# Half-word copies of 32 weight tiles moved to VectorE, units 4 to 9 turned by TensorE, new constants in the program's layout

## The chip, the cores and the metric

The kernel runs on one core of a Trainium2 chip. The metric is device time in microseconds (us) of one execution; the lower, the better. A core has a matrix engine (TensorE, PE in the rows; PEld is its weight load), VectorE (DVE), ScalarE (ACT), GpSimd (POOL) and SyncE (SP), which issues nearly all DMA transfers here. Each engine works through its own instructions in order.

## The reference

Three layers follow each other: attention over a window of 64 positions, a layer with squared relu, and a layer with a softmax gate and a normalization.

```python
# q, k, v: (4, 8, 576, 64)
scores = scale * q @ k^T;  mask: 0 <= i - j < 64
attn = softmax(scores) @ v                      # -> x: (2304, 512)
h = max(x @ w_in, 0);  x = h * h @ w_out        # (512, 2048), (2048, 512)
h = x @ w2_in                                   # (512, 1024)
s = h * softmax(h);  ln = (s - mean(s)) / sqrt(var(s) + 1e-6) * g_ln
out = ln @ w2_out                               # (1024, 512)
```

Activations are 32-bit floats. The four weight matrices come as 64-bit floats.

## The kernel before

**Weights.** A weight tile is 128 x 512. `assembled` loads its 64-bit words as they are (`load`, 512 KB, tile `wraw`), shifted by one 16-bit word, and makes 32-bit floats of them in two steps: `top` (L247, ScalarE) copies the highest half-word of each, read as bf16 and written as f16, into a word of the tile `top` (one of two that are used in turn) or straight into the result; `rest` (L250, VectorE) shifts the other bits and joins both. The 16 tiles of w_in (kind `a`, result `w`) and the 16 of w_out (kind `b`, result `wm`) go through `top`. For the second layer's weights (kinds `2i` and `2o`, 8 tiles each) GpSimd first clears the result (`home`, L235). `weights` then splits a tile into a high and a low part (L266 on ScalarE, L269 on VectorE), since each product is made of three (high times high and both mixed ones).

**Attention.** The 36 blocks of 64 positions are taken two at a time: 18 units. A unit is: load q and k (L372, L373), scores on TensorE (L418, `ps_s`), mask and maximum on VectorE (L421, L426), exponentials on ScalarE (L443), normalization (`norm`, L453, on VectorE for units 0 to 9 and on GpSimd after), a turn of the probabilities `e`, and the product with v (`values`, L511, `ps_v`). Units 0 to 3 are turned by TensorE (L471, `ps_p`) and copied out of PSUM by ScalarE (L489, `pt`). From unit 4 (`CROSSED = 4`) VectorE turns blocks of 32 x 32 (`blocks`, L477, tile `d`), and two transfers finish the turn through memory: `aside` (L480, 512 KB to `p_dram`) and `across` (L485, four of 128 KB into `pt`). From unit 4 on the result `xt` is stored (L533).

**Squared-relu layer.** Units 0 to 3 are pass 0: `ffn` multiplies by w_in (L688, `ps_h`) and w_out (L704, `ps_y`), hidden tile after hidden tile, while the later units run in between; 51 products without use (`ps_warm`, L1492) stand in the order early on. Units 4 to 9 are pass 2, units 10 to 17 pass 3. These use seven products in place of eight (`pair1`, L914, `ps_h`; sums `u2`, `u3`, `c22`, `c21`, `c12` on VectorE at L930, L934, L942, L945, L949, tiles `u1`, in rows `u` or `u_` with a number) for each pair j of hidden tiles. Their operands are sums and splits of x (`x_operands`) and of weights (`w_operands`, L854 to L867, tiles `ws`, `wo`, `wz`). `squares_of` squares on GpSimd (L622) and splits (L634 on ScalarE, L637 on VectorE); `second` multiplies by w_out (L1031). The hidden tiles go to memory and come back for the second half (`again_of`). The tag `wm` is a ring of four tiles, shared by `xt`, the sums and the weights of kind `b` and `2i`.

**Last layer.** `pair2` and `behind` (L1303, L1427 to L1449).

**Order.** All of this is laid out once, in Python: `add(engine, us, rank, function, after, take, give, port, late, at)` records a task, and `plan.run` picks again and again the task that could start first by these costs (ties by rank). `late` is what a transfer is assumed to take beyond its issue, `port` marks VectorE and GpSimd work that is assumed to exclude each other, `take` and `give` are slots of tiles. The result is a fixed order on each engine. On the chip only waits on data decide when an instruction of that order starts.

Of the kernel before, what the change touches and what calls it, by code (L numbers as in the profile page):

```python
# [26 lines left out]
class Plan:  # L27
# [71 lines left out]
def kernel(  # L99
# [92 lines left out]
    with ExitStack() as c1:  # L192
# [22 lines left out]
        def assembled(kind, i, rank, after=()):  # L215
            early = kind == "a" and i < EARLY
            ringed = kind in "ab"
            o = {}

            def load():  # L220
                o["raw"] = raw_p.tile([P, 1024], I32, tag="wraw", name="wraw", bufs=RAWS)
                nc.sync.dma_start(out=o["raw"].bitcast(U16)[:, : 4 * DM - 1], in_=SRC[kind][i][:, 1:])

            def home():
                if kind == "a":
                    if i // 2 not in w1:
                        w1[i // 2] = w1_p.tile([P, 2, 512], F32, tag="w1", name="w1")
                    o["m"] = w1[i // 2][:, i % 2]
                elif kind == "2o":
                    w2o[i] = w1_p.tile([P, 2, 512], F32R, tag="w1", name="w2o")  # L230
                    o["m"] = at_p.tile([P, 512], F32, tag="qk"[i % 2], name="w2m", bufs=1)
                else:
                    o["m"] = raw_p.tile([P, 512], F32, tag="wm", name="wm", bufs=WMB)
                if not ringed:
                    G.memset(o["m"], 0.0)  # L235

            def top():
                if ringed:
                    home()
                    if not tops:  # L240
                        tops.append(x_p.tile([P, 2, 512], F32, tag="xc", name="top", bufs=1))
                        G.memset(tops[0], 0.0)
                    o["t"] = tops[0][:, turns[0] % 2]
                    turns[0] += 1
                else:
                    o["t"] = o["m"]
                S.activation(out=o["t"].bitcast(F16)[:, 1::2], in_=o["raw"].bitcast(BF16)[:, 2::4], func=AF.Copy)  # L247

            def rest():
                V.scalar_tensor_tensor(out=o["m"].bitcast(I32), in0=o["raw"][:, ::2], scalar=13, in1=o["t"].bitcast(I32),  # L250
                                       op0=ALU.logical_shift_right, op1=ALU.bitwise_or)

            a = add("SP", 1.7, rank - (LEAD if early else 9), load, after, take=["raw"], late=2.0, at=0.7)
            own = {"a": [], "2o": ["qk"[i % 2] + "2"]}.get(kind, ["wm"])
            z = [] if ringed else [add("POOL", 0.6, rank - 9, home, after, take=own, port=True)]
            b = add("ACT", 0.57, rank, top, [a, *z], take=["top", *own] if ringed else [])
            return o, add("DVE", 0.62, rank, rest, [b], port=True, give=["raw", "top"] if ringed else ["raw"])

        def weights(kind, i, rank, after=()):
# [48 lines left out]
        def landed(lo, source, after, rank, n):  # L308

            def load():  # L310
                nc.sync.dma_start(out=lo[0]().bitcast(F32), in_=source())

            return add("SP", 0.8, rank - 6, load, [*after, *lo[2]], take=lo[1], late=2.2)

        def less(lo, a, b, after, rank, n, op=ALU.subtract):

# [22 lines left out]
        def attention(n, rank, after=()):  # L339
# [246 lines left out]
            else:  # L586
# [5 lines left out]
                    p = [add("PE", 0.85, rank, lambda: transposes(0), [*ns, before], take=["t", "t", "pt"], give=["e"])] * 2  # L592
                if crossed:
                    c = add("DVE", 1.2, rank, blocks, ns, take=["raw"], give=["e"], port=True)
                    c = add("SP", 0.8, rank, aside, [c], late=2.4, give=["raw"])
                    c = [add("SP", 1.6, rank, across, [c, before], take=["pt"], late=2.4)]
                else:
                    c = [add("ACT", 0.48, rank, lambda a=a: copied(a), [p[a]], give=["a" if begins else "t"]) for a in range(2)]
                p = add("PE", 1.15, rank, lambda: values(0), [*c, lv], take=["t"], give=["pt", vs])
                if t < 2:  # L600
                    h = add("ACT", 0.48, rank, lambda: high(0), [p])
                    x_ready[n] = add("DVE", 0.60, rank, lambda: rest(0), [h], give=["t"])
                else:
                    h = add("ACT", 0.48, rank, taken, [p], take=["wm"], give=["t"])
                    x_ready[n] = add("SP", 0.8, rank, store_x, [h], late=2.2, give=["wm"])
            p_after[n] = p


# [21 lines left out]
        def squares_of(o, N, rank, done, late=False, signed=True, turn=()):  # L630

            def high():
                o["g"] = g_p.tile([P, 2, NMAX], F32R, tag="g", name="g")
                S.activation(out=o["g"][:, 0, :N], in_=o["r"], func=AF.Copy)  # L634

            def rest():
                V.tensor_tensor(out=o["g"][:, 1, :N], in0=o["r"], in1=o["g"][:, 0, :N].bitcast(F32), op=ALU.subtract)  # L637

            e = squared(o, N, rank, done, late, signed)
            o["task"] = s = add("ACT", N / 1200 + 0.11, rank, high, [e, *turn], take=["g"])  # L640
            return add("DVE", N / 960 + 0.07, rank, rest, [s], port=True, give=[o["slot"]] if o["slot"] else [])
# [404 lines left out]
                        freed[dh] = got  # L1046
                        gone[t, half, dh] = got

        twin = {}

        def again_of(t, kk, at, unit, pos=None, last=None):
            N, half = HN[t], int(t > 1)
            base = next((b for b in TWINS if half and kk - b in (0, 1)), None)
            twice = base is not None
            o = {"slot": "raw" if twice else "wm" if kk > 3 and kk % 4 == 3 else "r"}
# [20 lines left out]
            else:  # L1076
# [2 lines left out]
                else:  # L1079
                    begun = [in_of[0, KF - 1 - AGO, 0]]  # L1080
                a = add("SP", 0.8, at - SOON - EARLIER, load, [r_ready[t, kk], *begun], take=[o["slot"]], late=3.5)
            e = squares_of(o, N, at - (FIRST if half and kk < 3 else SOON), [a], late=LATE_POOL and t == LAST, signed=None if half else False, turn=last_square[t][-2:][: 1 + kk] if half and kk < 2 else last_square.get(t, [])[-1:])
            if twice and kk > base:
                e["after"].append(twin["e"])
            twin["e"] = e
# [12 lines left out]
                return dict.__getitem__(self, k)  # L1098

        PAIR0, PAIR = 10.88, 8.6  # L1100
        JOIN, SECOND, MORE = 4, 0.17, PASSES[1]
        SKIP = 6 if MORE else KF

# [2 lines left out]
        V0, LATER, OUT = 3.12, 52.7, 4.55  # L1106
        LEAD = 14.41
        SOON, EARLIER, LATE_POOL = 25, 0, False
        PUT, PUT0, PUT1, AGO, LATEB, WOP = 16, 10, 3, 0, 145, 11
        TWINS, PAIRED, AHEAD, TWINJ = (3, 9), 2, 7, 7  # L1110
        NEXT, FIRST, ENDS = 20, 8, 70
        UNIT = (1.68, 2.12, 15.1, 22.97)
        WIDE, EAGER, CROSSED = 18, starts[3] // 2, 4
        W2I, W2O, XOP, KW = 11.0, 7.0, -15, 40
        NOT2I = lambda: first_of[2, 4]
        for n, (kind, kk) in enumerate((kind, kk) for kk in range(KF) for kind in "ab"):
            weights(kind, kk, LATEB + 3 * (kk - PUT) if kind == "b" and kk >= PUT else LOADS[n] if n < len(LOADS) else PAIR0 + PAIR * n / 2 - 2)
# [427 lines left out]
```

## Time and profile before

| | |
|---|---|
| median of 3 runs | 670.98 us (668.65 to 671.6) |
| profiled execution, its own time | 664.84 us |
| its span, first to last instruction | 662.8 us |
| TensorE busy | 634.9 us, 96% |
| VectorE busy | 494.8 us, 75% |
| ScalarE busy | 399.5 us, 60% |
| GpSimd busy | 129.6 us, 20% |

The profiled execution took 664.84 us, of which 2.0 us lie around the span. Of the span, TensorE stood still for 27.9 us, all but 5.2 us of it in the first 313 us.

### The profile page before, as it was taken

What the parts mean: (1) busy time and instruction counts of PE and PEld (TensorE: products, weight loads), DVE (VectorE), ACT (ScalarE), POOL (GpSimd) and SP (SyncE); (2) the same over time, 40 slices, a digit from 0 to 9 for tenths busy, and PEclk for the clock granted to TensorE, in tenths of its full rate; (3) what the DMA queues carried; (4) which work ended last, traced back from release to release, by engine and by line L of the source; (5) the groups of instructions that cost most, each with busy time, mean ns of one, the idle gap of its engine ahead of it and who ended that gap; (6) DMA issues with size and microseconds to landing.
All of it is one profiled execution on the core that took longest, in us unless ns stands there. A gap on an engine that the chain in (4) does not pass through costs nothing.

```text
span 662.8 us, 11290 instructions
## 1 busy us (share of the span) xinstructions
PE 634.9 (96%) x4041; PEld 532.4 (80%) x4041; DVE 494.8 (75%) x846; ACT 399.5 (60%) x899; POOL 129.6 (20%) x164
## 2 busy tenths in 40 slices
PE   8999998899898989999999999999999999999997
PEld 4678877688797889898888888888888787778786
DVE  5879878698985974379877674388888798787761
ACT  6877677658755833475555544564565666566652
POOL 1003022034324343101433333200000000000000
PEclk9999999999999989999999999999999999999999
DMA  8787998834878667765222113562165534565221
GB/s 285 262 309 249 285 321 297 257 105 146 267 221 262 211 199 227 266 238 167 84 87 92 66 64 142 193 202 67 49 189 176 183 116 125 149 191 157 105 72 48
DMA packets 75672, 118.18 MB, mean 178 GB/s; under 512 B 6880, under 2 KB 46304, under 8 KB 75616
## 3 DMA queue, kind: packets, MB, share of 16 engines
q1 hardware_dynamic: 75072, 117.20, 53.9%
q8 instruction: 32, 0.52, 0.3%
q10 hardware_dynamic: 544, 0.26, 0.1%
q14 instruction: 24, 0.20, 0.1%
HBM read 79.16 MB, written 38.27 MB: 177 GB/s over the span
## 4 chain that ended last, share of the span: by engine, by line
PE 48%; DVE 2%; DMA 1%; ACT 1%; issue 1%; SPq 0%; ACTq 0%; DVEq 0%
PE ps_o L1444 13%; PE ps_y L1031 13%; PE ps_h L1303 11%; PE ps_h L914 11%; DVE lnT L1437 1%; DMA l<-t_dram 1%; DVE e L1387 0%; DVE h L1404 0%; DVE nmax L1376 0%; ACT lnT L1433 0%; PE ps_lt L1427 0%; SPq L1413 0%; ACT h L1325 0%; ACT o L1449 0%; DVE h L1334 0%
## 5 line engine op out<-in xcount | busy, mean ns | idle before, releaser
L1031 PE MATMUL ps_y<-g,wb 128*128 128x384 f32 (+1 forms) x768 | 164.5, 363 | 1.9 <-ACT g L634 1.0
L1031 PEld LDWEIGHTS ps_y<-g,wb 128*128 128x128 f32 x768 | 138.6, 188 | 19.0 <-DVE g L637 2.0
L1444 PE MATMUL ps_o<-w2o,lnT 128*128 128x512 f32 x432 | 101.9, 393 | 1.3 <-DVE lnT L1437 1.3
L1444 PEld LDWEIGHTS ps_o<-w2o,lnT 128*128 128x128 f32 x432 | 80.5, 188 | 20.7 <-DVE lnT L1437 3.1
L622 POOL TENSOR_TENSOR r<-r 128x512 f32<-128x512 f32 (+2 forms) x36 | 41.0, 1142 | 185.8 <-ACT r L694 95.5
L622 POOL TENSOR_TENSOR u<-u 128x384 f32<-128x384 f32 (+1 forms) x48 | 48.1, 1006 | 85.2 <-ACT u L619 52.3
L637 DVE TENSOR_TENSOR g<-r,g 128x512 fp32r<-128x512 f32 (+2 forms) x68 | 44.4, 654 | 24.1 <-ACT g L634 24.0
L1303 PE MATMUL ps_h<-w2i,xx 128*128 128x512 f32 x243 | 62.4, 389 | 0.0
L634 ACT ACTIVATE g<-r 128x512 fp32r<-128x512 f32 (+2 forms) x68 | 38.1, 562 | 28.3 <-PE ps_y L1031 13.4
L914 PE MATMUL ps_h<-xb,wo 128*128 128x384 f32 (+1 forms) x192 | 50.9, 360 | 3.3 <-DVE u L930 2.1
L1303 PEld LDWEIGHTS ps_h<-w2i,xx 128*128 128x128 f32 x243 | 45.6, 188 | 9.5
L619 ACT ACTIVATE u<-u 128x384 f32<-128x384 f32 (+1 forms) x48 | 27.3, 575 | 42.0 <-DVE u L949 19.3
L914 PE MATMUL ps_h<-xa,wo 128*128 128x512 f32 (+1 forms) x192 | 51.8, 369 | 0.0
L704 PE MATMUL ps_y<-g,wb 128*128 128x512 f32 (+1 forms) x240 | 48.1, 353 | 1.5 <-ACT g L634 1.0
L443 ACT ACTIVATE e<-e,nmax 128x128 f32<-128x128 f32 x112 | 43.4, 390 | 8.4 <-DVE nmax L426 8.1
L688 PE MATMUL ps_h<-x,wa 128*128 128x512 f32 (+1 forms) x240 | 47.3, 351 | 0.3 <-ACT r L694 0.3
L914 PE MATMUL ps_h<-xo,wo 128*128 128x512 f32 (+1 forms) x128 | 47.5, 371 | 0.0
L704 PEld LDWEIGHTS ps_y<-g,wb 128*128 128x128 f32 x240 | 38.3, 189 | 8.5 <-ACT g L634 1.4
L688 PEld LDWEIGHTS ps_h<-x,wa 128*128 128x128 f32 x240 | 38.6, 189 | 7.6 <-PE ps_warm L1492 0.6
L1398 POOL TENSOR_SCALAR rstd<-rstd 128x1 f32<-128x1 f32 x18 | 3.5, 192 | 207.5 <-ACT e L1395 189.3
L914 PEld LDWEIGHTS ps_h<-xb,wo 128*128 128x128 f32 x192 | 34.2, 188 | 8.3 <-DVE u L930 2.7
L914 PEld LDWEIGHTS ps_h<-xa,wo 128*128 128x128 f32 x192 | 35.2, 188 | 5.3 <-DVE u L934 0.5
(153 smaller groups left out, 1148.7 us busy)
## 6 DMA issues: line engine op xcount, KB each, us to landing
wraw<-in_w_in SPq DMA_DIRECT2D x24, 511.8 KB, 5.0
wraw<-in_w_out SPq DMA_DIRECT2D x24, 511.8 KB, 5.5
vt<-in_v SPq DMA_DIRECT2D x32, 256.0 KB, 3.4
t_dram<-h SPq DMA_DIRECT2D x16, 512.0 KB, 2.6
l<-t_dram SPq DMA_DIRECT2D x64, 128.0 KB, 3.7
p_dram<-d SPq DMA_DIRECT2D x14, 512.0 KB, 4.1
pt<-p_dram SPq DMA_DIRECT2D x56, 128.0 KB, 4.0
kt<-in_k SPq DMA_DIRECT2D x16, 384.0 KB, 4.8
```

The lines of the kernel that those rows point to most:

```text
L443: S.activation(out=o["er"][:, a, w], in_=s, func=AF.Exp, scale=SCALE if begins else 1.0, bias=o["nmax"][:, a, w : w + 1], accum_out=o["sum ...
L619: S.activation(out=o["r"], in_=o["r"], func=AF.Relu)
L622: G.tensor_tensor(out=o["r"], in0=o["r"], in1=o["r"], op=ALU.mult)
L634: S.activation(out=o["g"][:, 0, :N], in_=o["r"], func=AF.Copy)
L637: V.tensor_tensor(out=o["g"][:, 1, :N], in0=o["r"], in1=o["g"][:, 0, :N].bitcast(F32), op=ALU.subtract)
L688: T.matmul(ps[:, :N], wa[kk][:, wi, c * P : c * P + P], xs[t][:, xi, c, n0:n1], start=n == 0, stop=n == 3 * DC - 1)
L704: T.matmul(acc[t, 0][d][:, n0:n1], wb[kk][:, wi, d * P : d * P + P], o["g"][:, xi, :N], start=kk == 0 and n == 0 and n0 == 0, stop=last an ...
L914: T.matmul(to[:, :N], w["t"][:, wi, off + c * P : off + c * P + P], (lo if xi else hi)()[:, c], start=begins and m == 0, stop=m == 5, skip ...
L1031: T.matmul(acc[t, half][d][:, :N], wb[kk][:, wi, d * P : d * P + P], q["g"][:, xi, :N], start=pos == 0 and n == 0, stop=pos == KF - 1 and ...
L1303: T.matmul(o[bank], o["xx", k][:, xi, at : at + P], w2i[w, r][wi][0](), start=begins and m == 0, stop=m == 5, skip_group_check=True)
L1437: V.tensor_tensor(out=parts2(l[:, 1]), in0=turned2(hf), in1=parts2(l[:, 0].bitcast(F32)), op=ALU.subtract)
L1444: T.matmul(o["o"], o["l", hf][:, xi, kk % 4, :], w2o[kk][:, wi, :], start=kk == 0 and n == 0, stop=kk == KF2 - 1 and n == 2)
```

## The change

Six things are changed; the computation stays the same.

1. The half-word copy of the 32 tiles of kinds `a` and `b` goes to VectorE (`V.tensor_copy`), assumed at 0.36 us and with `port`; for the second layer's weights it stays on ScalarE, assumed at 0.77 us in place of 0.57.
2. `CROSSED` becomes 10: units 4 to 9 are turned by TensorE and copied by ScalarE; units 10 to 17 still go through memory.
3. Transfers are assumed longer: weights 2.8 (was 2.0), operands of x 4.0 (2.2), the turn through memory 3.2 (2.4), stores of `xt` 2.8 (2.2).
4. The clearing of the second layer's tiles comes after their load, ranked 3 ahead of the copy (was 9 ahead and without the load).
5. At the start of the second half of passes 2 and 3 the first three squares read back wait for one square each of the first half, in a new order (`turn`).
6. Constants: `WOP` 13 (11), which ranks when operand sums may start; `ENDS` 80 (70), which packs units 10 to 17 earlier; `W2I` 8 (11) and `KW` 100 (40), which move the second layer's w_in tiles later.

```diff
             ringed = kind in "ab"
+            by_dve = ringed and i < TOPS
...
-                S.activation(out=o["t"].bitcast(F16)[:, 1::2], in_=o["raw"].bitcast(BF16)[:, 2::4], func=AF.Copy)
+                to, word = o["t"].bitcast(F16)[:, 1::2], o["raw"].bitcast(BF16)[:, 2::4]
+                if by_dve:
+                    V.tensor_copy(to, word)
+                else:
+                    S.activation(out=to, in_=word, func=AF.Copy)
...
-            a = add("SP", 1.7, rank - (LEAD if early else 9), load, after, take=["raw"], late=2.0, at=0.7)
+            a = add("SP", 1.7, rank - (LEAD if early else 9), load, after, take=["raw"], late=LATE, at=0.7)
...
-            z = [] if ringed else [add("POOL", 0.6, rank - 9, home, after, take=own, port=True)]
-            b = add("ACT", 0.57, rank, top, [a, *z], take=["top", *own] if ringed else [])
+            z = [] if ringed else [add("POOL", 0.6, rank - 3, home, [a], take=own, port=True)]
+            b = add(*(("DVE", 0.36) if by_dve else ("ACT", 0.77)), rank, top, [a, *z], take=["top", *own] if ringed else [], port=by_dve)
...
         def again_of(t, kk, at, unit, pos=None, last=None):
             N, half = HN[t], int(t > 1)
+            turn = last_square.get(t, [])[-1:]
+            if half and kk == 0:
+                ahead[t] = last_square[t][-2:]
+            if half and kk < 3:
+                turn = [*turn[: kk > 0], *ahead[t][kk == 2 :][:1]]
...
-        PUT, PUT0, PUT1, AGO, LATEB, WOP = 16, 10, 3, 0, 145, 11
+        PUT, PUT0, PUT1, AGO, LATEB, WOP = 16, 10, 3, 0, 145, 13
...
-        WIDE, EAGER, CROSSED = 18, starts[3] // 2, 4
-        W2I, W2O, XOP, KW = 11.0, 7.0, -15, 40
+        WIDE, EAGER, CROSSED = 18, starts[3] // 2, starts[3] // 2
+        W2I, W2O, XOP, KW = 8.0, 7.0, -15, 100
```

The order of the instructions is laid out anew by this, on all engines. Line numbers of the changed file are 5 to 11 higher. Three places:

VectorE, pass 0, where the tiles of weights are joined (`wm` and `w` are results of L250 before and of L255 now, `wb` and `wa` their low parts, `g` a split square). Before:

```order
L250 SCALAR_TENSOR_TENSOR wm<-wraw,top 128x512 x2
L250 SCALAR_TENSOR_TENSOR w_680<-wraw,top 128x512
L269 TENSOR_TENSOR wb<-wm,wb 128x512
L637 TENSOR_TENSOR g<-r,g 128x256
L269 TENSOR_TENSOR wb<-wm,wb 128x512
```

Now:

```order
L250 CAST top<-wraw 128x512
L642 TENSOR_TENSOR g<-r,g 128x256
L255 SCALAR_TENSOR_TENSOR wm<-wraw,top 128x512
L250 CAST top<-wraw 128x512 x2
L255 SCALAR_TENSOR_TENSOR wm<-wraw,top 128x512
L274 TENSOR_TENSOR wb<-wm,wb 128x512
L255 SCALAR_TENSOR_TENSOR w_724<-wraw,top 128x512
L274 TENSOR_TENSOR wb<-wm,wb 128x512
```

Each join now has its copy ahead of it on the same engine.

TensorE, the end of pass 0: the last two units ahead of pass 2, with their scores (`ps_s`) and values (`ps_v`) between the products of pass 0 (`ps_h` and `ps_y`). Before:

```order
L418 MATMUL ps_s<-kt,qt 64x128 x16
L704 MATMUL ps_y<-g,wb 128x512 x12
L511 MATMUL ps_v<-pt,vt 64x64 x16
L704 MATMUL ps_y<-g,wb 128x512 x12
L688 MATMUL ps_h<-x,wa 128x512 x36
L511 MATMUL ps_v<-pt,vt 64x64 x16
L704 MATMUL ps_y<-g,wb 128x512 x36
L511 MATMUL ps_v<-pt,vt 64x64 x16
```

Now:

```order
L423 MATMUL ps_s<-kt,qt 64x128 x16
L693 MATMUL ps_h<-x,wa 128x512 x24
L423 MATMUL ps_s<-kt,qt 64x128 x16
L693 MATMUL ps_h<-x,wa 128x512 x12
L476 MATMUL ps_p<-ident,e 128x128 x8
L693 MATMUL ps_h<-x,wa 128x512 x12
L519 MATMUL ps_v<-pt,vt 64x64 x16
L709 MATMUL ps_y<-g,wb 128x512 x12
L476 MATMUL ps_p<-ident,e 128x128 x8
L709 MATMUL ps_y<-g,wb 128x512 x12
L519 MATMUL ps_v<-pt,vt 64x64 x16
```

Eight turns (`ps_p`) stand ahead of each unit's values now, one run of twelve products before them; each of the six units 4 to 9 has such a row.

VectorE, pass 2, pair j = 6, from the sum `u3` (L934 before, L939 now) to the sum `c22` (L942 before, L947 now). Before:

```order
L934 TENSOR_TENSOR u_3032<-ps_h_1914,u_2995 128x384
L477 STREAM_TRANSPOSE d<-e 128x8x4x32
L637 TENSOR_TENSOR g<-u_2798,g 128x384
L448 TENSOR_SCALAR sums<-sums 128x2x4
L449 RECIPROCAL sums<-sums 128x2x4
L867 TENSOR_TENSOR wo<-w_1526,wo 128x512
L860 TENSOR_TENSOR ws<-w_1526,ws 128x256
L867 TENSOR_TENSOR wo<-ws,wo 128x512
L867 TENSOR_TENSOR wz<-w_1526,wz 128x256
L867 TENSOR_TENSOR wo<-ws,wo 128x512
L942 TENSOR_TENSOR u_3086<-ps_h_1915,u_3032 128x384
```

Now:

```order
L939 TENSOR_TENSOR u_3084<-ps_h_1946,u_3027 128x384
L255 SCALAR_TENSOR_TENSOR wm<-wraw,wm 128x512
L482 STREAM_TRANSPOSE d<-e 128x8x4x32
L872 TENSOR_TENSOR wo<-ws,wo 128x512
L947 TENSOR_TENSOR u_3115<-ps_h_1947,u_3084 128x384
```

Nine instructions stood between the two sums, and three do now.

## Rows read from the trace of the kernel before

**Rows 1.** Busy time by stretch: start:end, length, each engine, granted clock, DMA share, GB/s.

```profile
17.20:38.70 21.50, 20.96 (x235) 15.50 (x234) 18.64 (x40) 19.19 (x60) 2.40 (x4) 1.00 0.77 268
38.70:141.30 102.60, 95.28 (x797) 78.66 (x794) 83.86 (x131) 72.79 (x192) 18.26 (x17) 1.00 0.80 267
141.30:313.00 171.70, 160.19 (x1275) 148.03 (x1273) 130.08 (x217) 100.17 (x274) 55.23 (x60) 0.99 0.66 215
313.00:662.80 349.80, 344.61 (x1516) 282.56 (x1516) 252.26 (x430) 195.74 (x331) 51.09 (x73) 1.00 0.38 123
```

**Rows 2.** TensorE's waits from 38.7 to 141.3 us: total, times, longest.

```profile
PE ps_v L511 <- DMA pt<-p_dram: 4.0, 3, 1.9
PE ps_s L418 <- DMA kt<-in_k: 1.3, 1, 1.3
```

**Rows 3.** TensorE's waits from 141.3 to 313 us.

```profile
PE ps_h L914 <- DVE u L942: 2.4, 1, 2.4
PE ps_h L914 <- DVE u L930: 2.1, 2, 1.5
PE ps_s L418 <- DMA kt<-in_k: 2.1, 1, 2.1
PE ps_v L511 <- DMA pt<-p_dram: 1.3, 2, 0.8
PE ps_y L1031 <- ACT g L634: 1.0, 1, 1.0
```

**Rows 4.** Groups by line and form: count, busy us, mean ns, idle before.

```profile
L247 ACT ACTIVATE top<-wraw 128x512 f16<-128x512 bf16 x32 | 24.8, 788 | 15.4 <-DMA wraw<-in_w_in 13.0 <-DMA wraw<-in_w_out 2.1
L250 DVE SCALAR_TENSOR_TENSOR w<-wraw,top 128x512 int32<-128x512 int32 x16 | 10.9, 683 | 6.1 <-ACT top L247 6.1
L477 DVE STREAM_TRANSPOSE d<-e 128x1024 f32<-128x1024 f32 x14 | 17.3, 1235 | 0.3 <-POOL e L453 0.2
L489 ACT ACTIVATE pt<-ps_p 128x512 f32<-128x512 f32 x4 | 2.4, 592 | 0.0
```

**Rows 5.** The only VectorE copy with a change of type between SBUF tiles.

```profile
L172 DVE CAST ident_b<-ident x1: 241/241/241, 1.4 to 1.4; 128x128 bf16<-128x128 f32 x1
```

**Rows 6.** A run of eight TensorE turns, from the chain that ended last.

```profile
643.54 0.94 PE ps_lt L1427 x8
```

**Rows 7.** VectorE in order of time, normalizations of units 8 and 9: start, us, instruction.

```profile
96.05 1.29 DVE L453 TENSOR_TENSOR e<-e,sums 128x512 f32<-128x512 f32 x2
105.77 1.28 DVE L453 TENSOR_TENSOR e<-e,sums 128x512 f32<-128x512 f32 x2
```

**Rows 8.** TensorE in order of time: scores of units 8 and 9, and twelve products.

```profile
88.77 1.10 PE L418 MATMUL ps_s<-kt,qt 64*64 64x128 f32 x32
95.52 1.10 PE L418 MATMUL ps_s<-kt,qt 64*64 64x128 f32 x32
100.62 2.99 PE L704 MATMUL ps_y<-g,wb 128*128 128x512 f32 x12
```

**Rows 9.** Busy time by stretch again, and below it TensorE in order of time.

```profile
235.00:240.00 5.00, 3.40 (x11) 3.40 (x12) 3.13 (x7) 1.42 (x3) 0.83 (x1) 0.66 0.75 207
217.84 1.20 PE L914 MATMUL ps_h<-xa,wz 128*128 128x384 f32 x6
236.60 2.29 PE L914 MATMUL ps_h<-xa,wz 128*128 128x384 f32 x6 [2.38 <-DVE u L942]
```

**Rows 10.** VectorE and GpSimd in order of time, pass 2.

```profile
211.65 0.56 DVE L930 TENSOR_TENSOR u<-ps_h,p 128x384 f32<-128x384 f32 x1 [5.84 <-DMA xT_dram<-xt]
222.83 0.67 DVE L867 TENSOR_TENSOR wo<-ws,wo 128x512 fp32r<-128x512 f32 x1
233.62 1.52 DVE L867 TENSOR_TENSOR wo<-ws,wo 128x512 fp32r<-128x512 f32 x1
206.32 0.53 POOL L235 MEMSET wm<- 128x512 f32 x1 [1.75 <-DMA r_dram<-u]
232.11 2.49 POOL L453 TENSOR_TENSOR e<-e,sums 128x512 f32<-128x512 f32 x2 [0.44 <-DVE sums L449]
```

More of the change, by code (lines that the diff above doesn't have):

```diff
@@ L311, in load @@
                 nc.sync.dma_start(out=lo[0]().bitcast(F32), in_=source())
-            return add("SP", 0.8, rank - 6, load, [*after, *lo[2]], take=lo[1], late=2.2)
+            return add("SP", 0.8, rank - 6, load, [*after, *lo[2]], take=lo[1], late=LATE_X)
         def less(lo, a, b, after, rank, n, op=ALU.subtract):
@@ L594, in attention @@
                     c = add("DVE", 1.2, rank, blocks, ns, take=["raw"], give=["e"], port=True)
-                    c = add("SP", 0.8, rank, aside, [c], late=2.4, give=["raw"])
-                    c = [add("SP", 1.6, rank, across, [c, before], take=["pt"], late=2.4)]
+                    c = add("SP", 0.8, rank, aside, [c], late=LATE_P, give=["raw"])
+                    c = [add("SP", 1.6, rank, across, [c, before], take=["pt"], late=LATE_P)]
                 else:
@@ L604, in attention @@
                     h = add("ACT", 0.48, rank, taken, [p], take=["wm"], give=["t"])
-                    x_ready[n] = add("SP", 0.8, rank, store_x, [h], late=2.2, give=["wm"])
+                    x_ready[n] = add("SP", 0.8, rank, store_x, [h], late=2.8, give=["wm"])
             p_after[n] = p
@@ L1047, in second @@
                         gone[t, half, dh] = got
-        twin = {}
+        twin, ahead = {}, {}
         def again_of(t, kk, at, unit, pos=None, last=None):
             N, half = HN[t], int(t > 1)
+            turn = last_square.get(t, [])[-1:]
[3 more added lines that the diff above has]
+                turn = [*turn[: kk > 0], *ahead[t][kk == 2 :][:1]]
             base = next((b for b in TWINS if half and kk - b in (0, 1)), None)
@@ L1081, in again_of @@
                 a = add("SP", 0.8, at - SOON - EARLIER, load, [r_ready[t, kk], *begun], take=[o["slot"]], late=3.5)
-            e = squares_of(o, N, at - (FIRST if half and kk < 3 else SOON), [a], late=LATE_POOL and t == LAST, signed=None if half else False, turn=last_square[t][-2:][: 1 + kk] if half and kk < 2 else last_square.get(t, [])[-1:])
+            e = squares_of(o, N, at - (FIRST if half and kk < 3 else SOON), [a], late=LATE_POOL and t == LAST, signed=None if half else False, turn=turn)
             if twice and kk > base:
@@ L1100 @@
         PAIR0, PAIR = 10.88, 8.6
+        LATE, LATE_X, LATE_P, TOPS = 2.8, 4.0, 3.2, KF
         JOIN, SECOND, MORE = 4, 0.17, PASSES[1]
@@ L1108 @@
         SOON, EARLIER, LATE_POOL = 25, 0, False
-        PUT, PUT0, PUT1, AGO, LATEB, WOP = 16, 10, 3, 0, 145, 11
+        PUT, PUT0, PUT1, AGO, LATEB, WOP = 16, 10, 3, 0, 145, 13
         TWINS, PAIRED, AHEAD, TWINJ = (3, 9), 2, 7, 7
-        NEXT, FIRST, ENDS = 20, 8, 70
+        NEXT, FIRST, ENDS = 20, 8, 80
         UNIT = (1.68, 2.12, 15.1, 22.97)
-        WIDE, EAGER, CROSSED = 18, starts[3] // 2, 4
-        W2I, W2O, XOP, KW = 11.0, 7.0, -15, 40
+        WIDE, EAGER, CROSSED = 18, starts[3] // 2, starts[3] // 2
+        W2I, W2O, XOP, KW = 8.0, 7.0, -15, 100
         NOT2I = lambda: first_of[2, 4]
```

## The prediction

> **What bounds the kernel now.** I read the busy time by stretch first. From 313 us to the end TensorE is busy for 344.6 of 349.8 us at the full granted clock: nothing but less work on TensorE, or fewer of its waits, can shorten that stretch, and the change touches neither there. What can move lies ahead: 7.3 us in which TensorE stands still from 38.7 to 141.3 us (pass 0, with the attention of units 4 to 9 in between), and 11.5 us from 141.3 to 313 us (pass 2, with units 10 to 17) [rows 1]. From 17.2 to 38.7 us it is busy for 21.0 of 21.5 us, in part with the products without use; their number up to the first useful ones and after them is the same in both orders, so I give that stretch nothing. In both stretches that matter TensorE is the engine nearest to full, so I ask for each edit what it adds to TensorE and which of its waits it takes away. The lists of its waits say what those are: in pass 0 above all the probabilities that come back from memory (4.0 us in 3 waits) [rows 2], in pass 2 sums on VectorE, keys, probabilities and the split of a square [rows 3].
>
> **Half-word copies.** ScalarE loses 32 copies of 0.788 us, 25.2 us [rows 4]. VectorE gains 32, for which the trace has no row. From below: the one copy with a change of type, a quarter as wide, took 0.241 us [rows 5]. From above: the join of the same strided words, which reads two tiles, takes 0.683 us [rows 4]. I take the middle, 0.46 us, 14.7 us in all. The Trainium skill ("VectorE: DVE Perf Modes", The perf-mode tier table) gives a copy between SBUF tiles two elements per cycle even in 32 bits, and 1227 ns for 2048 of them; with its fixed part of some 150 cycles that would be an estimate of 0.42 us here. No run here shows it yet, and the sum below goes by the middle of the two rows.
>
> What hides it: from 17.2 to 141.3 us VectorE is busy for 18.6 + 83.9 = 102.5 of 124.1 us [rows 1]. It gains 14.7 us and loses six block turns of 1.235 us, 7.4 us [rows 4], so 109.8 us, 88%. It also no longer waits for ScalarE's copy ahead of a join (6.1 us before the joins of w_in) [rows 4]. At the upper price it would be 102.5 + 21.9 - 7.4 = 117.0 us, 94%, and the cover would be thin; that is a rival below. ScalarE goes from 92.0 to 92.0 - 25.2 + 7.1 = 73.9 us. I cost this edit at nothing.
>
> **Units 4 to 9 turned by TensorE.** Eight turns took 0.94 us [rows 6], so 5.6 us for six units, all on the engine that is the bound. ScalarE gets twelve copies of 0.592 us, 7.1 us [rows 4], in room that the first edit made. In return the 4.0 us of waits for probabilities from memory go, all of units 6, 8 and 9 [rows 2]. The 1.3 us wait for keys goes too, I think, since twelve transfers of 512 KB each leave that stretch, whose transfer engines are 80% busy [rows 1, 2]; I count 1.0 us, with ends of 0 and 1.3.
>
> The turn can wait in its place. From the scores to the end of the normalization it took 97.3 - 88.8 = 8.6 us for unit 8 and 107.05 - 95.5 = 11.5 us for unit 9 [rows 7, 8]. In the new order 36 products of pass 0 and the scores of the next unit stand between for the first of the two, and 36 products, a run of turns and one of values for the second; at 2.8 to 3.0 us for twelve [rows 8] that is 9.6 to 10.1 us and 10.5 to 11 us. So the first is covered and the second late by 0.5 to 1.0 us, if ScalarE is no faster than before; without its half-word copies it should be. I put down 0.5 us in all, with ends of 0 and 6 us (1.0 for each unit). Pass 0: 5.6 - 4.0 - 1.0 + 0.5 = **+1.1 us**, ends 0.3 (nothing waits anew, and the whole wait for keys goes) and +7.6.
>
> **Pass 2.** The longest wait there, 2.4 us, is for the sum `c22` [rows 3]. Ahead of it VectorE did nine other things after `u3`, one of them stretched beside GpSimd's normalization (1.52 us in place of 0.67) [rows 10]. In the new order three stand there for the same pair. By their usual times, some 2.6 us, this sum comes over 2 us sooner, so I let the whole wait go. With it goes what came behind it: the granted clock fell to 0.66 in that stretch, between full speed and the lower level, and six products took 2.29 us in place of 1.20 [rows 9]; 1.1 us. Together -3.5 us.
>
> The waits for `u2`, 2.1 us in two [rows 3], come from the ring of four `wm` tiles: VectorE stood for 5.84 us until a store of `xt` gave one back [rows 10]. GpSimd had just cleared and so taken one for a weight tile [rows 10]; now the clearing follows the load, and longer stores are assumed. That frees the ring for a while but not for certain: half, -1.0 us. The probabilities of units 10 to 17 still go through memory, but with 3.2 us assumed for each leg their values stand later in TensorE's order: -1.3 us. Keys, 2.1 us: half, -1.0. The square at the turn to the second half, 1.0 us, is what `turn` is about: -1.0. That makes -7.8 us. An order laid out anew also has waits of its own; TensorE stood still for 11.5 us here under the old order, and I put back 2.5 us. Pass 2: **-5.3 us**, ends -9 and +3.
>
> **The rest.** The second layer's w_in tiles move later, into pass 3, with eight copies on ScalarE and eight joins on VectorE, in a stretch where these are busy for 196 and 252 of 350 us [rows 1]: nothing. If that cover were gone, each would cost TensorE a wait of one join, 0.7 us, 5.5 us in all.
>
> **Sum.** +1.1 - 5.3 = -4.2 us: 660.6 us against the profiled execution's own 664.84. The median of the runs lies 6.1 us above that execution; the same difference gives **666.8 us**.
>
> **Rivals.**
> *The waits of pass 2 go and don't come back.* All of the 7.8 us, the small ones with them, and pass 0 at its lower end: -7.5 to -9.7 us, 662 us. For it speaks that the assumed costs come nearer to what the rows show (0.788 for a copy assumed at 0.57); against it that the ring and the queue of transfers stay as they were.
> *Nothing gained.* The waits of pass 2 come back at other places, and pass 0 pays its turns: -2 to +3 us, 671 us. For it speaks that units 10 to 17 still stand between the sums on VectorE, in the same number.
> *VectorE becomes the bound of pass 0: slower.* If the copy costs what the join does, VectorE is at 94%, and each of the six turns waits for its normalization as values waited for memory before, 1.3 us each, 8 us in place of the 0.5; pass 0 would cost 5.6 - 4.0 - 1.0 + 8 = 8.6 us. With -3 us in pass 2 that is +5.6 us, 676.6 us. It decides from about 1.1 us a unit. Against it speaks that ScalarE's load falls by a fifth, so that the exponentials between come sooner.
> *GpSimd and VectorE shut each other out.* VectorE's 0.67 us became 1.52 us beside GpSimd's normalization [rows 10]. If a copy is hit like that whenever GpSimd works, 18.3 of 102.6 us in pass 0 [rows 1], some six of 32 copies cost 0.85 us more, 5 us of VectorE's time; if half of it shows on TensorE, the gain shrinks to -1.7 us, 669.3 us. The Trainium skill ("SBUF — State Buffer", Who interferes with whom) says that of a VectorE instruction that uses both ports and a GpSimd instruction the first holds the ports for its whole length and the other one waits; by this, the trace agrees, with the 1.52 us.
>
> **How the numbers follow.** Forecast 0.42 (its own range 664 to 669), waits gone 0.18, nothing gained 0.17, shut out 0.08, slower 0.15. The range reaches from the first rival's lower end to near the slower one: **660 to 676 us**. A measurement of this kernel tells about 0.5%, 3.4 us, from no change. The forecast lies just beyond, so 0.28 of its 0.42 count as faster; with the 0.18 of the waits gone and 0.02 of the others that is 0.48 faster; 0.36 the same (0.14 of the forecast, 0.15 of nothing gained, 0.07 of shut out); 0.16 slower.
>
> **What would show it.** In the changed kernel's profile the copies would be rows of 0.4 to 0.5 us on VectorE, the 48 turns 5.6 us of TensorE, and no wait for probabilities from memory would stand ahead of the first product of pass 2, which would start within 2 us of 141.3. The time between that product and the last stretch would be some 5 us shorter, with no 2 us wait for `c22`, and the granted clock would stay at its full level there. The prediction is wrong if TensorE waits for its turns by over a microsecond a unit, if copies take as long as joins, or if pass 2 shows as much idle time as before.

## The result and the profile after

The changed kernel took 651.36 us in the median of 4 runs (650.79 to 655.35), the kernel before 669.82 us in the same comparison: a ratio of 0.974, 95% interval 0.969 to 0.979. Forecast were 666.8 us and 660 to 676. The direction was right; the gain is 18.5 us where 4.2 were forecast, and the time lies below the range.

The profiled execution of the changed kernel took 651.62 us, 13.2 us less than that of before. First the busy time by stretch, changed kernel. I cut at two marks of TensorE's order: the first product of pass 2 (139.80 us after, 141.27 before) and the first of pass 3 (301.6 and 314.6). Columns as in [rows 1].

```profile
0.00:38.70 38.70, 36.01 (x464) 24.12 (x465) 30.92 (x79) 24.12 (x93) 5.01 (x15) 1.00 0.82 272
38.70:139.80 101.10, 99.88 (x838) 83.03 (x837) 88.23 (x152) 65.08 (x183) 17.68 (x16) 1.00 0.63 211
139.80:301.60 161.80, 157.52 (x1281) 148.15 (x1280) 126.81 (x213) 99.01 (x273) 52.27 (x55) 1.00 0.67 216
301.60:649.80 348.20, 342.53 (x1511) 281.27 (x1509) 255.30 (x432) 197.58 (x333) 55.90 (x78) 1.00 0.41 130
```

The kernel before, cut at the same marks:

```profile
38.70:141.27 102.57, 95.25 (x797) 78.63 (x793) 83.83 (x131) 72.76 (x192) 18.23 (x17) 1.00 0.81 267
141.27:314.60 173.33, 161.67 (x1281) 149.29 (x1280) 131.71 (x220) 101.60 (x276) 55.26 (x60) 0.99 0.66 217
```

The last stretch is 348.2 us in both. Pass 2 runs the same products (1281 records in each) in 161.80 us in place of 173.33, and up to it 1.5 us are saved although TensorE does more. So 11.5 of 13.0 us come from pass 2. There TensorE stands still for 161.80 - 157.52 = 4.3 us in place of 11.7, and is busy for 4.2 us less with the same work. Its waits in the changed kernel, from 38.7 us to the first product of pass 2 (the first two lines) and in pass 2 (the others):

```profile
PE ps_s L423 <- DMA kt<-in_k: 0.8, 1, 0.8
PE ps_p L476 <- DVE e L458: 0.3, 1, 0.3
...
PE ps_s L423 <- DMA kt<-in_k: 1.0, 1, 1.0
PE ps_v L516 <- DVE nmax L431: 0.7, 1, 0.7
PE ps_h L919 <- DVE u L950: 0.7, 1, 0.7
PE ps_y L1036 <- DVE g L642: 0.7, 1, 0.7
PE ps_v L516 <- DMA pt<-p_dram: 0.6, 1, 0.6
PE ps_v L516 <- DMA r_dram<-u: 0.4, 1, 0.4
```

Against [rows 2, 3] the waits for probabilities in pass 0 are gone, and so are those for `c22` (2.4 us) and `u2` (2.1). The moved work, groups by line and form:

```profile
L250 DVE CAST top<-wraw 128x512 f16<-128x512 bf16 x32 | 13.9, 467 | 0.0
L494 ACT ACTIVATE pt<-ps_p 128x512 f32<-128x512 f32 x16 | 9.1, 595 | 3.4 <-PE ps_p L476 3.2
L476 PE MATMUL ps_p<-ident,e 128*128 128x128 f32 x64 | 9.2, 276 | 0.8 <-DVE e L458 0.6
```

The lines show the copies on VectorE, the copies of turned probabilities on ScalarE and the turns on TensorE. A half-word copy costs 0.467 us in the mean (0.456 in the median), the forecast was 0.46; 48 of the 64 turns are new. The last two units ahead of pass 2, in TensorE's order of time:

```profile
102.27 1.03 PE L476 MATMUL ps_p<-ident,e 128*128 128x128 f32 x8
103.06 2.99 PE L693 MATMUL ps_h<-x,wa 128*128 128x512 f32 x12
105.99 1.15 PE L519 MATMUL ps_v<-pt,vt 128*64 128x64 f32 x32
...
109.93 0.60 PE L476 MATMUL ps_p<-ident,e 128*128 128x128 f32 x4
110.84 0.63 PE L476 MATMUL ps_p<-ident,e 128*128 128x128 f32 x4 [0.31 <-DVE e L458]
```

Only one turn waited, 0.31 us, that of the second unit.

### The profile page after: what moved, and what is told of

The parts are those of the page before. It is cut to its first block, busy times and chain, and to the rows that moved or that the text cites. A ratio compares the mean times of both kernels' runs of the same rounds, so it can differ in the third digit from the quotient of the medians.

```text
span 649.8 us, 11333 instructions
## 1 busy us (share of the span) xinstructions
PE 635.9 (98%) x4089; PEld 536.6 (83%) x4089; DVE 501.3 (77%) x872; ACT 385.8 (59%) x879; POOL 130.9 (20%) x164
## 4 chain that ended last, share of the span: by engine, by line
PE 62%; DVE 5%; DMA 4%; ACT 3%; SPq 2%; issue 1%; ACTq 0%; DVEq 0%
PE ps_y L1036 22%; PE ps_h L919 17%; PE ps_o L1455 12%; PE ps_h L1314 10%; DMA l<-t_dram 1%; PE ps_v L516 1%; DMA pt<-p_dram 1%; SPq L1424 1%; DVE e L1398 1%; DMA p_dram<-d 1%; ACT o L1460 1%; ACT e L1406 1%; ACT e L448 1%; DVE wo L872 1%; DVE lnT L1448 1%
## 5 line engine op out<-in xcount | busy, mean ns | idle before, releaser
L1455 PE MATMUL ps_o<-w2o,lnT 128*128 128x512 f32 x432 | 100.4, 390 | 0.2 <-DVE lnT L1448 0.2
L627 POOL TENSOR_TENSOR r<-r 128x512 f32<-128x512 f32 (+2 forms) x36 | 39.0, 1086 | 194.6 <-ACT r L699 116.8
L642 DVE TENSOR_TENSOR g<-r,g 128x512 fp32r<-128x512 f32 (+2 forms) x68 | 42.6, 627 | 28.1 <-ACT g L639 27.5
L627 POOL TENSOR_TENSOR u<-u 128x384 f32<-128x384 f32 (+1 forms) x48 | 47.9, 1003 | 77.9 <-ACT u L624 45.3
L1409 POOL TENSOR_SCALAR rstd<-rstd 128x1 f32<-128x1 f32 x18 | 5.5, 307 | 203.3 <-ACT e L1406 185.2
L1314 PE MATMUL ps_h<-w2x,xx 128*128 128x512 f32 x135 | 36.8, 392 | 1.8 <-ACT p L1320 1.8
```

The source lines that it names most:

```text
L627: G.tensor_tensor(out=o["r"], in0=o["r"], in1=o["r"], op=ALU.mult)
L1314: T.matmul(o[bank], o["xx", k][:, xi, at : at + P], w2i[w, r][wi][0](), start=begins and m == 0, stop=m == 5, skip_group_check=True)
L1455: T.matmul(o["o"], o["l", hf][:, xi, kk % 4, :], w2o[kk][:, wi, :], start=kk == 0 and n == 0, stop=kk == KF2 - 1 and n == 2)
```

## The experiments

Four theories came first. **A**: the numbers of the layout carry the gain. **B**: the moved work carries it. **C**: the order before is an unlucky one, and any new one moves the time by a few us. **D**: the two need each other. Later came **E** (the assumed price of the copy), **F** (the assumed transfer times), **G** (the clearing of tiles) and **H** (the constants), and for the last question **K** (the turns pay by keeping TensorE busy) and **M** (they pay by sparing the trip through memory). All ran against the kernel before on the same chip, whose median lay between 667.9 and 669.8 us; so the ratios are what is compared. Their intervals reach some 0.3 to 0.5% to either side, 2 to 3 us. "Pass 2 from" is its first product, "pass 2" its length, both in the profiled execution, in us; the clock is the mean granted to TensorE over the whole of that execution.

| run | median us | ratio, interval | pass 2 from | pass 2 | clock |
|---|---|---|---|---|---|
| before, 1st and 2nd profile | | 1 | 141.3, 144.6 | 173.3, 173.5 | 0.997, 0.994 |
| after | 651.36 | 0.974, 0.969 to 0.979 | 139.8 | 161.8 | 0.999 |
| a_act | 656.93 | 0.983, 0.979 to 0.987 | 141.2 | 165.1 | 0.999 |
| a_mem | 655.99 | 0.981, 0.978 to 0.985 | 140.1 | 168.4 | 0.992 |
| a_const | 652.42 | 0.976, 0.972 to 0.980 | 139.1 | 161.9 | 0.999 |
| a_late | 656.21 | 0.982, 0.979 to 0.986 | 141.5 | 164.6 | 0.997 |
| a_turn | 650.95 | 0.973, 0.969 to 0.977 | 139.8 | 161.2 | 1.000 |
| a_home | 653.83 | 0.977, 0.974 to 0.981 | 140.3 | 167.7 | 0.997 |
| a_layout | 655.59 | 0.979, 0.976 to 0.983 | 143.4 | 164.7 | 0.997 |
| b_both | 658.61 | 0.985, 0.982 to 0.988 | 141.2 | 166.4 | 1.000 |
| b_copies | 665.82 | 0.995, 0.992 to 0.997 | 144.7 | 168.0 | 0.995 |
| b_pe | 664.57 | 0.993, 0.991 to 0.996 | 141.7 | 172.7 | 0.997 |
| b_cost | 666.68 | 0.997, 0.994 to 1.000 | 141.9 | 172.6 | 0.992 |
| b_late | 662.68 | 0.989, 0.985 to 0.993 | 137.7 | 172.9 | 0.992 |
| b_home | 666.45 | 0.995, 0.992 to 0.998 | 143.9 | 173.1 | 0.992 |
| b_const | 665.38 | 0.997, 0.994 to 0.999 | 144.3 | 173.5 | 0.995 |
| b_late_home | 659.04 | 0.986, 0.982 to 0.989 | 139.5 | 170.9 | 0.994 |
| a_fill | 659.40 | 0.985, 0.982 to 0.989 | 146.3 | 164.8 | 0.997 |
| a_turn46 | 655.73 | 0.980, 0.977 to 0.983 | 143.1 | 164.1 | 1.000 |

**One part undone in the changed kernel (names with a_).**

The copies back on ScalarE:

```diff
-        LATE, LATE_X, LATE_P, TOPS = 2.8, 4.0, 3.2, KF
+        LATE, LATE_X, LATE_P, TOPS = 2.8, 4.0, 3.2, 0
```

> The changed kernel with the 32 half-word copies back on ScalarE (assumed at 0.77 us there). Theory A, the layout carries the gain: the constants and the assumed transfer times took the waits of pass 2 away, the copies only make room in pass 0. Then this costs 1 to 3 us against the changed kernel's 651.4, all before the first product of pass 2 (139.8 us): 652.5 to 654.5 us. Theory B, the moved work carries it: with ScalarE relieved everything runs ahead, in pass 2 too; then 658 us or more. Theory C, any new order would do: within 3 us either way, at no particular place.

656.93 us lies between A and B. Pass 2 starts 1.4 us later and is 3.3 us longer, though none of the 32 copies runs in it (the last starts at 114.3 us in the changed kernel, at 109.5 us here). So what is lost there must come by way of the order that is laid out around the copies; its longest wait there is 2.6 us at scores, for `wo` from VectorE.

Units 4 to 9 through memory again:

```diff
-        WIDE, EAGER, CROSSED = 18, starts[3] // 2, starts[3] // 2
+        WIDE, EAGER, CROSSED = 18, starts[3] // 2, 4
```

> The changed kernel with units 4 to 9 turned through memory again. Theory A: TensorE loses 5.6 us of turns and gets back waits for probabilities and keys of 4 to 7 us in pass 0; 650 to 653.5 us, pass 2 as in the changed kernel. Theory B: the twelve transfers of 512 KB fill the queue again and what follows is late as well; 656 us or more. Theory C: as A, with waits at new places of pass 2.

655.99 us, at the edge of B. Pass 2 starts as early as with the turns, so up to there the 5.6 us of turns are made up by waits and a lower clock (0.98). But they are not the waits that A named: none is for probabilities, 0.6 us are for keys, and 3.6 us for parts of weights and split squares. Pass 2 is 6.6 us longer, in part at a lower clock (0.98 there too).

The old constants:

```diff
-        PUT, PUT0, PUT1, AGO, LATEB, WOP = 16, 10, 3, 0, 145, 13
+        PUT, PUT0, PUT1, AGO, LATEB, WOP = 16, 10, 3, 0, 145, 11
-        NEXT, FIRST, ENDS = 20, 8, 80
+        NEXT, FIRST, ENDS = 20, 8, 70
-        W2I, W2O, XOP, KW = 8.0, 7.0, -15, 100
+        W2I, W2O, XOP, KW = 11.0, 7.0, -15, 40
```

> The changed kernel with the old constants (ranks of operand sums, of units 10 to 17 and of the second layer's w_in tiles). Theory A: 3 to 7 us of TensorE's waits come back between the first product of pass 2 and the first of pass 3, 655 to 659 us, among them waits for sums u on VectorE. Theory B: under 2 us more, 651 to 653.5 us. Theory C: 2 to 4 us more, with waits that are not those of before.

652.42 us and the same pass 2: B's number, and A's 655 to 659 us is missed. With the rest changed, the constants bring nothing that this shows.

The old transfer times (2.0, 2.2, 2.4 and 2.2):

> The changed kernel with the old assumed transfer times (weights 2.0, operands of x 2.2, turn through memory 2.4, stores of xt 2.2). Theory A: waits for what transfers bring or free (keys, probabilities, u behind the store of xt) come back, 2 to 4 us, 653.5 to 655.5 us. Theory B: under 1 us. Theory C: 2 to 4 us more, with waits that are not for transfers.

656.21 us, a little more than A says. Of the two long waits in pass 2 one is for a transfer (2.2 us before values), one for a split square (1.9 us).

The old order of squares, and the old clearing (`rank - 9, home, after` for `rank - 3, home, [a]`):

> The changed kernel with the old order of squares at the turn to the second half. My prediction's step: 1 us more, a wait for a split square of the second half of pass 2: 652 to 653 us. Theory C: 1 to 5 us more, at other places.

> The changed kernel with the old clearing of the second layer's tiles (9 ahead, without the load). My prediction's step: up to 1 us more, a wait for a sum behind the store of xt: 651.5 to 652.5 us. Theory C: 1 to 5 us more, at other places.

`turn` is worth nothing here: 650.95 us, where I had 1 us for it. Undoing the clearing costs 2.5 us by the medians, but the two intervals overlap (0.974 to 0.981 and 0.969 to 0.979), so the price is not clear of the noise. What is clear is that the mechanism of [rows 10] comes back. VectorE's waits with the clearing undone:

```profile
DVE u L947 <- DMA xT_dram<-xt: 3.9, 2, 2.5
DVE u L939 <- DMA xT_dram<-xt: 2.3, 1, 2.3
```

The changed kernel has no such wait for a store. TensorE waits 1.3 us for `c22` again.

**The layout without the moved work, and the moved work without the layout.** a_layout makes the edits of a_act and a_mem together; b_both puts the copies on VectorE and `CROSSED = starts[3] // 2` into the kernel before, b_copies and b_pe one of the two.

> The changed layout alone: copies on ScalarE and units 4 to 9 through memory, as before, all else as in the changed kernel. Theory A, the layout carries most: half or more of the 17 us gain, 660 us or less, pass 2 (first of its products to first of pass 3) under 168 us. Theory B, the moved work carries it: 664 to 668 us, pass 2 over 170 us, waits for probabilities back in pass 0. Theory D, layout and moved work need each other (the single undoings cost about 5 us each): 660 to 664 us.

> The kernel before with both moves of work (copies on VectorE, units 4 to 9 turned by TensorE) and the old layout numbers. Theory A: only pass 0 gains its 1 to 2 us, 665 to 668 us, pass 2 stays at some 173 us. Theory B: 653 to 657 us, pass 2 under 165 us. Theory D: 658 to 664 us.

> The kernel before with the copies on VectorE alone. Theory A: 666 to 668 us, within 1 us of before in each stretch. Theory B: 661 to 665 us. Theory D: 664 to 668 us, waits for probabilities from memory in pass 0 as before (3 to 5 us).

> The kernel before with units 4 to 9 turned by TensorE alone; ScalarE keeps its 25 us of half-word copies and gets 7 us of copies out of PSUM. Theory A: 667 to 670 us. Theory B: 661 to 665 us, pass 2 faster because the queue of transfers is emptier at its start. Theory D: 664 to 668 us, with ScalarE over 90% busy from 38.7 us to the first product of pass 2 and waits of TensorE for it.

The layout alone gives 13.8 of the 18.5 us, as A says; but the moved work alone gives 10.7, more than A allows. Together they give less than the sum, as they would if they take away, in part, the same waits. Nor do they need each other, as D has it: b_both lies in D's range (658 to 664 us), but a_layout lies 4 us below it. b_copies shows the price of the copies under the old layout: the waits for probabilities in pass 0 are gone, and TensorE waits 3.0 us for the part of `wa` that ScalarE makes and 2.4 us for VectorE's part in their place. So D's number fits b_copies (664 to 668 us), but not its sign, the waits for probabilities. b_pe lies where both B and D had it, and neither sign shows: pass 2 is not faster (172.7 us), and ScalarE is not short ahead of it, busy for 77.9 of 103.0 us (76%). In pass 2 TensorE waits 3.7 us for a split square from ScalarE.

**One layout edit on the kernel before.** b_cost: ScalarE's copy assumed at 0.77 us; b_late: the transfer times; b_home: the clearing; b_const: the constants; b_late_home: two of them.

```diff
-            b = add("ACT", 0.57, rank, top, [a, *z], take=["top", *own] if ringed else [])
+            b = add("ACT", 0.77, rank, top, [a, *z], take=["top", *own] if ringed else [])
```

> The kernel before with one number changed: ScalarE's half-word copy is assumed at 0.77 us in the layout in place of 0.57. Theory E, the order of pass 2 suffers from copies that take longer than the layout assumes (25.2 us in place of 18.2 on ScalarE): 658 to 664 us, pass 2 (first of its products to first of pass 3) under 169 us. Theory F, the transfer times are what the order lacked: 666 to 670 us, pass 2 at 171 to 174 us. Theory C, the order before is merely an unlucky one and most others are better: 661 to 667 us, and so each of these four runs on its own.

> The kernel before with only the assumed transfer times changed (weights 2.8, operands of x 4.0, turn through memory 3.2, stores of xt 2.8). Theory F: 657 to 662 us, pass 2 under 168 us, and less waiting for keys, probabilities and the sums behind the stores of xt. Theory E: 666 to 670 us. Theory C: 661 to 667 us.

> The kernel before with only the clearing of the second layer's tiles changed (after the load, 3 ahead). Theory G, GpSimd's early clearing takes wm tiles from the ring of four, so that sums on VectorE wait for stores of xt, and that is what pass 2 pays: 660 to 664 us, pass 2 under 169 us, no wait of VectorE's sums for the store of xt. Theory H, the constants do it: 667 to 670 us, pass 2 over 171 us. Theory C, any new order: 661 to 667 us with other waits in place of these.

> The kernel before with only the constants changed (ranks of operand sums, of units 10 to 17, of the second layer's w_in tiles). Theory H: 658 to 663 us, pass 2 under 168 us. Theory G: 667 to 670 us, waits of VectorE's sums for the store of xt as before. Theory C: 661 to 667 us.

> The kernel before with the transfer times and the clearing changed. Theory G: the two add up, 662.7 of the transfer times alone less 4 to 7 us, 655.5 to 659 us, near the whole layout's 655.6. Theory H: within 1.5 us of the transfer times alone, 661 to 664 us. Theory C: 658 to 664 us.

E falls with b_cost (pass 2 stays at 172.6). F nearly has the size (5.7 us by the medians, 662.68 us where 657 to 662 was expected) and is wrong in place: b_late gains ahead of pass 2 and leaves pass 2 at 172.9. There its granted clock is 0.97, in place of 0.99 before, behind a wait of 3.8 us for `xo`; by an estimate from that clock (0.03 of 172.9 us) some 5 us of this pass 2 are lower clock, so what the transfer times spare there may be hidden by it. H is wrong too: the constants alone leave pass 2 at 173.5. C is not refuted by any of the four: each lies in its 661 to 667 us, and every other order that was tried, in all the runs here, was faster than the one before. What C does not give is the 13.8 us of the whole layout. G is right on VectorE and wrong on the time. With the clearing alone VectorE's waits for stores of `xt` fall from 5.8 + 2.1 us to

```profile
DVE u L934 <- DMA xT_dram<-xt: 0.3, 1, 0.3
```

and TensorE's waits for sums shrink, but pass 2 is as long as before. TensorE's waits in pass 2 of b_home:

```profile
PE ps_v L511 <- DMA pt<-p_dram: 7.4, 5, 3.3
PE ps_s L418 <- DMA kt<-in_k: 2.6, 1, 2.6
PE ps_y L1031 <- DVE g L637: 0.9, 1, 0.9
PE ps_h L914 <- DVE u L945: 0.7, 1, 0.7
PE ps_h L914 <- DVE u L930: 0.5, 1, 0.5
```

The probabilities that come through memory, 1.3 us of waiting in [rows 3], now take 7.4, so what stood behind the sums seems to come out. b_late_home, with longer transfers assumed as well, waits 1.6 us for them, and 5.9 us for operands of x (`xo`, `xb`) in their place; it gains what the two ratios multiplied would give (0.984; measured 0.986), and lies between G's range (655.5 to 659 us) and the middle of C's (658 to 664), so it doesn't tell the two apart.

**The kernel before, profiled a second time.**

> The kernel before once more, for a second profile. If single executions differ by how long TensorE runs at the lower clock, the stages of this execution differ from the first in the granted clock and by the time that it explains; if they differ by waits for transfers, in those waits.

This execution took 669.25 us, near the median. Its stretches from 38.7 us to the first product of pass 2, and pass 2:

```profile
38.70:144.60 105.90, 97.52 (x806) 80.23 (x803) 83.97 (x131) 72.89 (x192) 18.51 (x17) 0.98 0.78 257
144.60:318.10 173.50, 160.96 (x1282) 149.37 (x1281) 133.20 (x220) 101.55 (x277) 54.40 (x60) 0.99 0.66 217
```

It is 4.6 us longer than the first: 3.3 ahead of pass 2, 0.2 in it, 1.1 after it. Both the clock (0.98 in place of 1.00 ahead of pass 2) and waits differ: there TensorE waits 1.8 us for `g` from ScalarE (1.0 in the first profile) and 1.1 us for `r` (0.3). Set against this execution, the changed kernel's gain is 17.6 us and no longer 13.2: 4.8 ahead of pass 2, 11.7 in it, 1.1 after it.

**What the turns are worth.** In a_fill units 4 to 9 go through memory as in a_mem, and TensorE turns the identity, without use, eight times for each of them ahead of its values; in the text on record "halves" means these products.

```diff
+                    if n < starts[3] // 2:
+                        add("PE", 0.85, rank, fill, ns, take=["t", "t"], give=["t", "t"])
...
+            def fill():
+                for b in range(2):
+                    ps = ps_t.tile([P, HP, W], F32, tag="t", name="ps_f")
+                    for w in range(HP):
+                        T.transpose(ps[:, w, :], ident, ident)
```

> The changed kernel with units 4 to 9 turned through memory again, and for each of them sixteen halves of work without use on TensorE in place of its turn: eight products of the identity in the same spot of its order (48 in all, 5.6 us). Output as before. Theory K, the turns paid by keeping TensorE busy and its clock up: as fast as the changed kernel or nearly so, 651 to 654 us, mean granted clock 0.997 or more. Theory M, the trip through memory is what cost: no faster than the same kernel without the useless work (656.0), 656 to 661 us, and waits for what comes from memory.

659.40 us, in M's range. Against a_mem pass 2 starts 6.2 us later, so the useless work does not fit into the waits, and the granted clock ahead of pass 2 is 0.98 in both; against the changed kernel, with about the same work on TensorE, the trip through memory costs 8.0 us. So far as one run tells, the turns pay by that trip, not by keeping TensorE busy. (How far the next run puts such a difference in doubt is said there.)

**A nearer price.** a_turn46 is a_turn with VectorE's copy assumed at the 0.46 us that it takes.

> The changed kernel with the old order of squares at the turn, and with VectorE's copy assumed at the 0.46 us that it takes in place of 0.36. Theory E, prices nearer to the chip's make a better order: 648 to 651 us. Theory C, any new order moves the time by a few us either way: 650 to 655 us.

655.73 us: E falls once more. A single assumed number, 0.10 us, costs 4.8 us by the medians against a_turn (650.95). The profiled executions differ by 5.9 us, 3.3 us ahead of pass 2 and 2.9 in it. One such case does not measure the scatter of the layout, but it shows that it can be as large as what a_act, a_mem or a_late show; a_fill's 8.0 us are more. No run beat the changed kernel beyond its interval.

## Why the prediction was wrong

The mechanism was right in the main: waits of TensorE go, and the moved work is covered. What failed is the size of four terms of the sum: in pass 2 the 2.5 us put back (about nothing, net, by the trace) and the 1.1 us for the clock (busy time fell by 4.2), the 6.1 us carried over to the median (-0.3 measured), and pass 0 at +1.1 us (-1.5 measured).

**Half-word copies: price right, gain missed.** 0.46 us was forecast and 0.456 measured in the median. That the middle between 0.24 and 0.68 us came out so closely is luck as well as working. VectorE did not become the bound; from 38.7 us to pass 2 it is busy for 88.23 of 101.10 us, 87% (88% forecast, from 17.2 us on). The estimate of 0.42 us from the Trainium skill ("VectorE: DVE Perf Modes", The perf-mode tier table) lies 0.04 us below the median copy and meets the fastest, 0.417 us. But I gave this edit no gain. In pass 0 the waits for ScalarE's `g` and `r` (1.0 and 0.3 us before) are gone, and ahead of 38.7 us, where I gave nothing, TensorE stands still for 2.7 us in place of 3.8 (busy for 34.86 of 38.70 us before; 35.65 in its second profile). That ScalarE's relief did it is argued, not shown: in a_act, with the copies back on ScalarE, 0.2 us of these waits return, and in a_turn46, with the copies on VectorE, TensorE waits 1.5 us for `g`.

**The turns: right in the main.** There are 48 new turns, no wait for probabilities, and 0.3 us of new waiting (0.5 forecast). TensorE waits 0.8 us for keys (0.3 forecast). From 38.7 us to the first product of pass 2 TensorE stands still for 1.2 us in place of 7.3, 6.1 less where I had 4.5 less; with the 1.1 us at the start and 5.8 us more of work up to pass 2 that makes the -1.5 us, in place of +1.1.

**Pass 2: what I let go did go; what I put back did not come.** Of the five waits that I named, 6.7 us were to go and 7.3 did (`c22` 2.4, `u2` 2.1, keys 1.1, the split square 1.0, probabilities 0.7). The step that failed is "I put back 2.5 us": TensorE stands still 7.4 us less in all, so what came new (0.7 us for a maximum, 0.4 for a store of hidden tiles) is no more than the small waits that went. The clock's term failed as well: 1.1 us forecast, while busy time fell by 4.2. Of this some 1.7 us are the lower clock (an estimate from [rows 9]: 0.34 of 5.00 us were not granted there); the rest I can only argue: after most waits the next product takes 0.44 us in place of 0.33 to its end, and there are fewer waits. Pass 2 came to -11.5 where I had -5.3.

**Why it went is only half settled.** That the early clearing takes tiles from the ring and makes VectorE's sums wait for stores, as I read from [rows 10], is shown by a_home and b_home. That this pays only when the probabilities behind it are early is what b_home suggests; it is not shown. None of the four layout edits that were tried alone shortens pass 2 by as much as a microsecond (172.6 to 173.5 us), and two of them bring it to 170.9; the whole layout brings 164.7, the moved work 166.4. The copies alone bring 168.0, though pass 2 starts 3.4 us later with them, and the turns alone 172.7. Which combination does it stays open, since one assumed number moves the time by 4.8 us: the shares of the edits can't be told apart more finely than that.

**The last step of the sum was the dearest.** "The same difference gives 666.8" carried 6.1 us, by which the median of before lay above its profiled execution, over to the changed kernel. Its median lies 0.3 us below its profiled execution, so this step alone is wrong by 6.4 us, pass 2 by 6.2, pass 0 by 2.6: together 15.2 of the 15.4 us by which the forecast was off; the rest is rounding and what lies outside these stretches.

Luck has a part in this step. Of the 86 other executions of the kernel before that were timed next to these kernels (662.99 to 673.59 us), three took 664.84 us or less: the profiled execution was an unusually fast one. Its rows left out waits that an ordinary execution has. In the second profile of before, 4.6 us longer, these were waits for ScalarE and a lower clock, above all ahead of pass 2, and the changed kernel takes most of that away too. But the change doesn't take the spread away: its own four runs reach from 650.79 to 655.35 us, and over the other kernels here the profiled execution lay anywhere from 4.1 us below the median to 2.8 above it. Such a difference belongs to the one execution and can't be carried from kernel to kernel.

**The rivals.** "The waits of pass 2 go and don't come back" was the mechanism that happened. Its 662 us lacked the same last step, and the 7.5 to 9.7 us that it gave as gain are still short of the 13.2 between the profiled executions. VectorE as the bound did not show. Nor did the shutting out cost the copies much: three of the 32 overlap work of GpSimd, and one of these took 0.87 us; the other 31 took under 0.5. Other work of VectorE was hit: the two normalizations of a unit, 1.28 us alone, took 2.12 to 2.98 us beside GpSimd's squares in the five last of the six units 4 to 9, and of this only the 0.31 us above reached TensorE as a wait for its turns.

## What to carry to other kernels

Before adding the difference between a median and a profiled execution to a sum, see where the profiled execution lies among the others, and profile a second one: the rows of a fast execution leave out waits that the usual one has, and a change may take those away as well. A wait taken away shows the next one behind it, so edits that do nothing alone can be worth something together, and each must be tried in the company that it will have. Where the order comes from a table of assumed prices, try neighbouring values before crediting an edit with a few us: here 0.10 us in one price changed the time by 4.8 us.

## What the runs showed of the hardware that I had not expected

A long wait of TensorE can cost more than its length, since its granted clock can be lower for a while behind it. In [rows 9] there were 2.38 us of waiting, a granted clock of 0.66 in that stretch, and six products at 2.29 us in place of 1.20. The same shows in a_fill (the first three lines) and in the second profile of before (the other three). The first two of each three are TensorE in order of time, the third is the busy time of four us behind the wait, columns as in [rows 1].

```profile
113.56 1.15 PE L522 MATMUL ps_v<-pt,vt 128*64 128x64 f32 x32 [3.50 <-DMA kt<-in_k]
114.64 4.60 PE L717 MATMUL ps_y<-g,wb 128*128 128x512 f32 x12
116.00:120.00 4.00, 4.00 (x13) 3.15 (x13) 2.40 (x4) 0.78 (x2) 0.00 (x0) 0.69 0.92 288
```

```profile
116.35 1.72 PE L511 MATMUL ps_v<-pt,vt 128*64 128x64 f32 x32 [1.99 <-DMA pt<-p_dram]
118.00 3.30 PE L704 MATMUL ps_y<-g,wb 128*128 128x512 f32 x9
116.00:120.00 4.00, 3.65 (x37) 3.18 (x38) 3.29 (x4) 2.14 (x5) 1.36 (x1) 0.59 0.92 243
```

Twelve products took 4.60 us behind the first wait, where twelve took 2.99 in [rows 8]. From 38.7 us to pass 2 the granted clock was 1.00 in all nine kernels that turn units 4 to 9 on TensorE, and 0.97 or 0.98 in eight of the eleven profiles in which these units go through memory. It isn't each long wait: in a_act TensorE waited 2.6 us at one place, and the mean clock of that execution is 0.999. But in the three cases above the products behind a wait took 1.1 to 1.6 us more than at the full clock, on top of the wait itself; the forecast counted this for one wait alone.
